# Decode attention over cached keys and values plus a gated MLP: a key load in two transfers, another place for the products with the values, and a finer cut of an output weight

## The chip, the cores and the metric

The kernel runs on one core of a Trainium2 chip. The metric is device time in microseconds (us) of one execution; the kernel before took 668.58, 668.60 and 669.65 us in three timed runs (median 668.6). A separate execution was profiled; its trace is what the views below are taken from.

## The reference

Four decode tokens (batch 4, one position each, width 640) are layer-normalised. Attention with 32 heads of width 128 runs over a cache of 4096 keys and values per head, and a gated MLP over the same normalised input; both results are added to `x`.

```python
def _A_ref(x, k_cache, v_cache, wq, wo):        # x: (4, 1, 640), caches: (4, 32, 4096, 128)
    q = (x @ wq).reshape(B, Sq, Hq, Dh).transpose(0, 2, 1, 3)
    scores = jnp.einsum('bhqd,bhkd->bhqk', q, k) * Dh ** (-0.5)
    p = _softmax(scores, axis=-1)
    o = jnp.einsum('bhqk,bhkd->bhqd', p, v)
    return o.transpose(0, 2, 1, 3).reshape(B, Sq, Hq * Dh) @ wo
...
xn = _layernorm(x, axis=-1)
return x + _A_ref(xn, A_k_cache, A_v_cache, A_wq, A_wo) + _B_ref(xn, B_w_in, B_w_sp, B_b_sp, B_w_out)
```

All tensors are bf16. The two caches are 134 MB each, so almost all of the 282 MB that the kernel reads is keys and values, each read once.

## The kernel before

**Tiles.** The work is cut into `NT` = 16 steps, one for each of four groups of eight heads and each batch. One step's keys are one SBUF tile of 128 partitions x 256 positions x 128 values (`NC` = 256), 8.39 MB, loaded by one transfer (`load_k`, L118); its values are a tile of the same size (`load_v`, L123). Key tiles have two buffers (pool `kp`), value tiles one (pool `vp`). The first key buffer to be used holds `wq` at the start; the value buffer holds the MLP's weights (`w_sb`) at the start and `wo` at the end. The last step's values go to a key buffer as `v_last`, in three transfers.

**One step.** A key tile is worked off in four parts of 64 positions (`NU` = 4). For each part, VectorE multiplies the keys in place by the query (`product`, L402, the line L403), folds the two halves of the 128 products together (`fold`, L410, line L412), TensorE adds up eight slices by eight matmuls against the identity (`sums`, L416, line L421), and VectorE reduces what stands in PSUM to scores (`row_sums`, L429, line L432). The step's softmax is done during the next step: maximum, exponential on ScalarE (`exps`, L488), then on VectorE the spreading of the probabilities into one column block per head (`own_heads`, L497, line L499, tile `pm`), and on TensorE 64 matmuls of `pm` with the value tile (`weighted`, L508, line L514, tile `pv`). `take` (L524) copies the result to SBUF and `diag` (L534) picks each head's rows. After each fourth step a group of heads is divided by its sum and turned (`group_den`, `group_rows`, `group_turn`). At the end `group_proj` multiplies the four groups by the four blocks of `wo` (line L592).

**Order.** The order on TensorE, VectorE, ScalarE and SyncE is the order in which the code calls these functions (`tc.manual_schedule`, L609); nothing is moved by a planner. SyncE issues all large transfers in that order, and a transfer is issued when its buffer is free. In step i, the values of step i are issued after `weighted(i - 1)` has read the one value buffer, and the keys of step i + 2 after the fourth `sums` of step i has read its key buffer. The compiled program counts the landings of its transfers on eight semaphores in turn, so that an issue also waits for the transfer eight issues before it.

**The end.** In the last step the four blocks of `wo` (1280 KB each) are issued in the place of the next values: the first three in one transfer each, the last in four pieces (`WO_CUTS`, L133: 640, 320, 160 and 160 KB). The order on TensorE is then: products with `v_last`, `group_proj(0)`, `diag`, `group_proj(1)`, `group_turn`, `group_proj(2)`, and `group_proj` of the last block in four pieces (L674).

Of the kernel before, what the change touches and what calls it, by code (L numbers as in the profile page):

```python
# [17 lines left out]
def kernel(  # L18
# [14 lines left out]
    nc = tc.nc  # L33
    P = nc.NUM_PARTITIONS
    Bsz, Sq, D = A_x.shape
    _, H, S, Dh = A_k_cache.shape
# [9 lines left out]
    HG = H // HT  # L46
    NT = HG * Bsz
    LN = P // HT
    NC = HT * S // P
# [10 lines left out]
    WJ = HT * Dh // P  # L60
# [19 lines left out]
    def k_slot(name):  # L80
        return kp.tile([P, SLOT], BF16, tag="k", name=name)

    def v_slot(name):
        return vp.tile([P, SLOT], BF16, tag="v", name=name)
# [20 lines left out]
        out=w_out_sb[:, 0:NFF, :], in_=B_w_out[0 : NFF * P].rearrange("(p k) n -> p k n", k=NFF)  # L105
# [3 lines left out]
    def kv_view(cache, i):  # L109
        hg, b = divmod(i, Bsz)  # L110
        return cache[b, HT * hg : HT * (hg + 1)].rearrange("h s d -> (h s) d").rearrange(
            "(p c) d -> p (c d)", c=NC
        )
# [3 lines left out]

    def load_k(i):  # L118
        t = k_slot("k_nat")
        nc.sync.dma_start(out=t[:], in_=kv_view(A_k_cache, i))  # L120
        k_tiles[i] = t[:].rearrange("p (c d) -> p c d", d=Dh)

    def load_v(i, t):  # L123
        cuts = V_CUTS if i == NT - 1 else (0, NC)
        for c0, c1 in zip(cuts, cuts[1:]):
            nc.sync.dma_start(
                out=t[:, c0 * Dh : c1 * Dh], in_=kv_view(A_v_cache, i)[:, c0 * Dh : c1 * Dh]
            )
        v_tiles[i] = t[:].rearrange("p (c d) -> p c d", d=Dh)

    wo_v = A_wo.rearrange("(g p j) n -> g p j n", p=P, j=WJ)
    wo_t = []
    WO_CUTS = (0, 4, 6, 7, WJ)  # L133

    def load_wo():
        t = v_slot("wo")[:, 0 : HG * WJ * D].rearrange("p (g j n) -> p g j n", g=HG, n=D)
        wo_t.append(t)
        for g in range(HG):
            cuts = WO_CUTS if g == HG - 1 else (0, WJ)
            for j0, j1 in zip(cuts, cuts[1:]):  # L140
                nc.sync.dma_start(out=t[:, g, j0:j1, :], in_=wo_v[g][:, j0:j1, :])  # L141

    load_k(0)


# [18 lines left out]
    for i in range(NSTAT):  # L164
# [5 lines left out]
        out=rstd[:], in_=mv[:, 1:2], func=ACT.Sqrt, bias=eps_tile[:Bsz], scale=1.0  # L170
# [3 lines left out]
        out=xn_bf,  # L174
# [9 lines left out]
    for c in range(DC):  # L184
        nc.tensor.transpose(
            out=xnT_ps[:, c, :], in_=xn_v[:, c, :], identity=ident[:Bsz, :Bsz]
# [7 lines left out]
    def out_sum(half):  # L194
        return out_ps[OG * half : OG * half + Bsz, :]

    for half in range(2):
        nc.tensor.matmul(
            out=out_sum(half),
# [9 lines left out]
        out=own[:], in_=ident_f[:].rearrange("p (h l) -> p h l", h=HT), axis=AX.X, op=ALU.add  # L209
# [4 lines left out]
        out=pick[:, :, GW - HT : GW],  # L214
        in_=ident_f[:].rearrange("p (j h c) -> p c h j", c=CB, h=HT),
# [5 lines left out]
        out=row_head_f[:],  # L221
        in_=ident_f[:ROWS, :ROWS].rearrange("p (b h) -> p h b", h=HT),
# [5 lines left out]
        out=row_head[:], in_=row_head_f[:, :, None].to_broadcast([ROWS, HT, LN])  # L228
# [3 lines left out]
        out=row_batch_f[:],  # L232
        in_=ident_f[:ROWS, :ROWS].rearrange("p (b h) -> p b h", h=HT),
# [8 lines left out]
    for h in range(H):  # L242
        for c in range(DC):
            nc.tensor.matmul(  # L244
                out=q_ps[:, h, :],
# [6 lines left out]
    nc.vector.tensor_copy(out=qT[:], in_=q_ps[:])  # L252

    load_k(1)


# [124 lines left out]
    def stage_q(i):  # L381
        hg, b = divmod(i, Bsz)
        q_l = small.tile([P, HT, LN], BF16, name="q_l", bufs=1)
        nc.scalar.copy(  # L384
            out=q_l[:],
            in_=qT[:, HT * hg : HT * (hg + 1), b : b + 1].to_broadcast([P, HT, LN]),
        )
        qb_ps = ps_m.tile([P, Dh], FP32, tag="m", name="qbc_ps")
        nc.tensor.matmul(  # L389
            out=qb_ps[:],  # L390
            lhsT=q_l[:].rearrange("p h l -> p (h l)"),
            rhs=ident[:],
            start=True,
            stop=True,
        )
        qbcs[i] = small.tile([P, Dh], BF16, name="qbc")
        nc.scalar.copy(out=qbcs[i][:], in_=qb_ps[:])

    def part(i, u):
        return k_tiles[i][:, u * UC : (u + 1) * UC, :]  # L400

    def product(i, u):  # L402
        nc.vector.tensor_tensor(  # L403
            out=part(i, u),
            in0=part(i, u),
            in1=qbcs[i][:, None, :].to_broadcast([P, UC, Dh]),
            op=ALU.mult,
        )

    def fold(i, u):  # L410
        t = part(i, u)
        nc.vector.tensor_tensor(  # L412
            out=t[:, :, 0:HD2], in0=t[:, :, 0:HD2], in1=t[:, :, HD2:Dh], op=ALU.add
        )

    def sums(i, u):  # L416
        t = part(i, u)
        s = sums_ps[i, u] = ps_s.tile([P, UC, RW], FP32, name="s_ps")
        n = HD2 // RW
        for g in range(n):  # L420
            nc.tensor.matmul(  # L421
                out=s[:],
                lhsT=ident[:],
                rhs=t[:, :, g * RW : (g + 1) * RW],
                start=(g == 0),
                stop=(g == n - 1),
            )

    def row_sums(i, u):  # L429
        if u == 0:  # L430
            scores[i] = small.tile([P, NC], FP32, name="s_sb", bufs=1)
        nc.vector.tensor_reduce(  # L432
            out=scores[i][:, u * UC : (u + 1) * UC],
            in_=sums_ps.pop((i, u))[:],
            axis=AX.X,
            op=ALU.add,
        )
# [148 lines left out]
        oTs[hg] = const.tile([P, WJ, Bsz], BF16, name=f"oT{hg}")  # L586
        nc.scalar.copy(out=oTs[hg][:], in_=t_ps[:])

    def group_proj(hg, j0=0, j1=WJ):
        for j in range(j0, j1):  # L590
            for half in range(2):
                nc.tensor.matmul(  # L592
                    out=out_sum(half),
                    lhsT=oTs[hg][:, j, :],
                    rhs=wo_t[0][:, hg, j, half * NOH : (half + 1) * NOH],
                    start=False,
                    stop=(hg == HG - 1 and j == WJ - 1),
                )

    def at(i, fn, *args):  # L600
        if 0 <= i < NT:
            fn(i, *args)

    def group(i, fn):
        if 0 <= i < NT and i % Bsz == Bsz - 1:
            fn(i // Bsz)

    E = mybir.EngineType
    with tc.manual_schedule(engines={E.PE, E.DVE, E.Activation, E.SP}):  # L609
        stage_q(0)  # L610
        gmlp()
        load_v(0, v_slot("v_nat"))
        for i in range(NT):
            product(i, 0)
            fold(i, 0)
            at(i - 1, row_sums, NU - 1)
            at(i - 1, lane_max)
            group(i - 2, group_rows)
            sums(i, 0)
            at(i - 1, turn_max)  # L620
            group(i - 2, group_turn)
            product(i, 1)
            at(i - 1, head_max)
            at(i - 1, spread_max)
            fold(i, 1)
            at(i - 1, bias)
            at(i - 1, exps)
            at(i + 1, stage_q)
            sums(i, 1)
            row_sums(i, 0)  # L630
            product(i, 2)
            at(i - 1, own_heads)
            fold(i, 2)
            sums(i, 2)
            row_sums(i, 1)
            at(i - 1, weighted)
            if i == 0:
                pass
            elif i < NT - 1:
                load_v(i, v_slot("v_nat"))  # L640
            else:
                load_wo()
            at(i - 1, take)
            product(i, 3)
            fold(i, 3)
            sums(i, 3)
            row_sums(i, 2)
            if i + 2 < NT:
                load_k(i + 2)
            elif i + 2 == NT:  # L650
                load_v(NT - 1, k_slot("v_last"))
            at(i - 1, diag)
            group(i - 1, group_den)
        L = NT - 1
        row_sums(L, NU - 1)
        lane_max(L)
        group(L - 1, group_rows)
        turn_max(L)
        head_max(L)
        spread_max(L)  # L660
        bias(L)
        exps(L)
        own_heads(L)
        for c0, c1 in zip(V_CUTS, V_CUTS[1:]):
            weighted(L, c0, c1)
        take(L)
        group_den(HG - 1)
        group_proj(0)
        diag(L)
        group_rows(HG - 1)  # L670
        group_proj(1)
        group_turn(HG - 1)
        group_proj(2)
        for j0, j1 in zip(WO_CUTS, WO_CUTS[1:]):  # L674
            group_proj(HG - 1, j0, j1)

        res = small.tile([P, NOH], BF16, tag="two_k", name="res")
        out_v = out.flatten_outer_dims()
        r0, r1 = slice(0, Bsz), slice(OG, OG + Bsz)
        nc.scalar.copy(out=res[r0], in_=out_ps[r0])  # L680
        nc.vector.tensor_copy(out=res[r1], in_=out_ps[r1])
        nc.scalar.dma_start(out=out_v[:, 0:NOH], in_=res[r0])
        nc.sync.dma_start(out=out_v[:, NOH:D], in_=res[r1])
# [30 lines left out]
```

## Time and profile before

| | |
|---|---|
| timed runs | 668.58, 668.60, 669.65 us |
| profiled execution | 669.53 us, of which the span from first to last instruction is 667.8 us |
| VectorE busy | 505.9 us (76%) |
| TensorE matmul busy | 312.8 us (47%) |
| ScalarE busy | 33.6 us (5%) |
| SyncE's DMA queue (q1) | 282.24 MB, busy for 98.2% of the 16 engines' span |
| read from HBM | 282.24 MB, 423 GB/s over the span |
| L403 `product` | 64 of 4417 ns, 282.7 us; idle before them 100.3 us, all of it for key transfers |
| L421 `sums` | 512 matmuls, 201.6 us |
| L412 `fold` | 64 of 2285 ns, 146.2 us |
| L514 `weighted` | 960 matmuls with `v_nat`, 60.8 us |

The busy time of an engine says how much it did, not whether the end waited for it. Which one the end waited for is read from the chain of waits that ended last, and from the share and the rate of the DMA engines in slices of the span. A busy matmul is not TensorE at its peak, since matmuls are pipelined.

### The profile page before, as it was taken

The numbers are of one execution on the slowest core, as the hardware profiler recorded it, in microseconds if no ns is written. First come the engines' busy times: TensorE is split into PE (matmuls) and PEld (weight loads), VectorE is DVE, ScalarE is ACT, GpSimd is POOL, SyncE is SP. The second block draws the span as 40 slices with busy tenths as digits, with TensorE's granted clock in tenths as the row PEclk, the third lists the DMA queues.
The fourth block names the chain that finished last, engine by engine and source line by source line (L and its number), as shares of the span: only waits on it lengthen the run. The fifth ranks groups of instructions, "written<-read, shape, count | busy, mean of one in ns | idle before, by whom it ended". The sixth has DMA issues, their size and how long they took to land.

```text
span 667.8 us, 4772 instructions
## 1 busy us (share of the span) xinstructions
PE 312.8 (47%) x2089; PEld 128.7 (19%) x2089; DVE 505.9 (76%) x328; ACT 33.6 (5%) x93; POOL 1.0 (0%) x8
## 2 busy tenths in 40 slices
PE   0605546524626335462734446272434626444467
PEld 0501112211202112120211212121111212111123
DVE  1239999939689596968969596996949699695971
ACT  0200000000000000000000000000000000000000
POOL 0000000000000000000000000000000000000000
PEclk9999978575766778576665857666576755768688
DMA  9999997999999999999999999999999999999996
GB/s 372 448 437 440 417 412 315 440 437 440 433 436 416 416 441 436 436 433 440 437 432 436 437 420 433 432 424 433 440 437 432 436 440 425 432 436 425 418 417 263
DMA packets 6497, 282.56 MB, mean 423 GB/s; under 512 B 736, under 2 KB 1100, under 8 KB 1484
## 3 DMA queue, kind: packets, MB, share of 16 engines
q1 hardware_dynamic: 6456, 282.24, 98.2%
q8 instruction: 16, 0.26, 0.2%
q14 instruction: 5, 0.04, 0.0%
q10 hardware_dynamic: 20, 0.01, 0.0%
HBM read 282.24 MB, written 0.01 MB: 423 GB/s over the span
## 4 chain that ended last, share of the span: by engine, by line
DMA 54%; DVE 33%; PE 11%; ACT 1%; issue 1%; SPq 1%; DVEq 0%
DMA k_nat<-in_A_k_cache_dram 51%; DVE k_nat L403 19%; DVE k_nat L412 9%; PE s_ps L421 6%; PE pv L514 4%; DMA wo<-in_A_wo_dram 2%; DVE s_sb L432 2%; DVE pm L499 1%; ACT p L488 1%; PE out_ps L592 1%; DVE m L441 1%; DVE wide L565 0%; DVE o_n L559 0%; DVE nm L451 0%; SPq L141 0%
## 5 line engine op out<-in xcount | busy, mean ns | idle before, releaser
L403 DVE TENSOR_TENSOR k_nat<-k_nat,qbc 128x8192 bf16<-128x8192 bf16 x64 | 282.7, 4417 | 100.3 <-DMA k_nat<-in_A_k_cache_dram 100.3
L421 PE MATMUL s_ps<-k_nat,ident 128*128 128x512 bf16 x512 | 201.6, 565 | 257.4 <-DVE k_nat L412 257.4
L412 DVE TENSOR_TENSOR k_nat<-k_nat 128x4096 bf16<-128x4096 bf16 x64 | 146.2, 2285 | 1.2
L421 PEld LDWEIGHTS <-ident 128*128 128x128 bf16 x512 | 65.6, 131 | 371.0 <-issue 285.1
L514 PE MATMUL pv<-v_nat,pm 128*32 128x512 bf16 x960 | 60.8, 410 | 0.0
L432 DVE TENSOR_REDUCE s_sb<-s_ps 128x64 f32<-128x512 f32 x64 | 43.8, 685 | 11.4 <-ACT p L488 10.0
L514 PEld LDWEIGHTS <-pm 128*32 128x32 bf16 x1024 | 26.9, 104 | 45.9 <-issue 22.8
L462 PE MATMUL nb_ps<-nm,ones_row 1*128 1x8 f32 x32 | 7.3, 297 | 32.3 <-DVE nm L451 32.3
L488 ACT ACTIVATE p<-s_sb,nb 128x256 bf16<-128x256 f32 x16 | 8.1, 507 | 279.1 <-DVE nb_h L470 279.1
L389 PE MATMUL qbc_ps<-ident,q_l 128*128 128x128 bf16 x16 | 4.6, 289 | 37.3 <-ACT q_l L384 37.3
L524 ACT COPY e<-pv 128x512 f32<-128x512 f32 x16 | 9.4, 586 | 235.9 <-PE pv L514 229.2
L499 DVE TENSOR_TENSOR pm<-p,own_c 128x2048 bf16<-128x2048 bf16 x16 | 19.5, 1219 | 0.7 <-ACT p L488 0.7
L534 PE MATMUL o_ps<-e,pick 128*32 128x128 f32 x128 | 17.0, 275 | 0.0
L534 PEld LDWEIGHTS o_ps<-e,pick 128*32 128x32 f32 x128 | 12.8, 109 | 6.4 <-issue 6.4
L462 PEld LDWEIGHTS nb_ps<-nm,ones_row 1*128 1x128 f32 x32 | 5.9, 228 | 40.6 <-DVE nm L451 28.6
L252 DVE CAST qT<-q_ps 128x128 bf16<-128x128 f32 x1 | 0.3, 292 | 14.8 <-PE q_ps L244 14.8
L555 DVE RECIPROCAL rden<-den 32x1 f32<-32x1 f32 x4 | 0.6, 156 | 12.5 <-PE den L551 12.5
L244 PE MATMUL q_ps<-xnT,wq 128*128 128x4 bf16 x160 | 4.4, 166 | 11.1 <-DMA wq<-in_A_wq_dram 11.1
L389 PEld LDWEIGHTS <-q_l 128*128 128x128 bf16 x16 | 1.7, 106 | 39.0 <-ACT q_l L384 38.7
L592 PE MATMUL out_ps<-wo,oT 128*4 128x320 bf16 x64 | 6.4, 363 | 1.7 <-DMA wo<-in_A_wo_dram 1.7
L441 DVE TENSOR_REDUCE m<-s_sb 128x1 f32<-128x256 f32 x16 | 6.7, 420 | 0.6
L244 PEld LDWEIGHTS <-wq 128*128 128x128 bf16 x160 | 4.3, 104 | 11.5 <-DMA wq<-in_A_wq_dram 11.5
(85 smaller groups left out, 76.9 us busy)
## 6 DMA issues: line engine op xcount, KB each, us to landing
wq<-in_A_wq_dram SPq DMA_DIRECT2D x1, 5120.0 KB
v_last<-in_A_v_cache_dram SPq DMA_DIRECT2D x1, 4096.0 KB, 34.3
v_last<-in_A_v_cache_dram SPq DMA_DIRECT2D x2, 2048.0 KB, 38.9
wo<-in_A_wo_dram SPq DMA_DIRECT2D x3, 1280.0 KB
w_sb<-in_B_w_in_dram SPq DMA_DIRECT2D x1, 2160.0 KB, 20.1
w_sb<-in_B_w_out_dram SPq DMA_DIRECT2D x1, 960.0 KB, 22.7
wo<-in_A_wo_dram SPq DMA_DIRECT2D x1, 640.0 KB, 16.6
wo<-in_A_wo_dram SPq DMA_DIRECT2D x1, 320.0 KB, 17.0
```

Of the source, the lines that this page charges most:

```text
L403: nc.vector.tensor_tensor(out=part(i, u), in0=part(i, u), in1=qbcs[i][:, None, :].to_broadcast([P, UC, Dh]), op=ALU.mult,)
L412: nc.vector.tensor_tensor(out=t[:, :, 0:HD2], in0=t[:, :, 0:HD2], in1=t[:, :, HD2:Dh], op=ALU.add)
L421: nc.tensor.matmul(out=s[:], lhsT=ident[:], rhs=t[:, :, g * RW : (g + 1) * RW], start=(g == 0), stop=(g == n - 1),)
L432: nc.vector.tensor_reduce(out=scores[i][:, u * UC : (u + 1) * UC], in_=sums_ps.pop((i, u))[:], axis=AX.X, op=ALU.add,)
L441: nc.vector.tensor_reduce(out=m1[:], in_=scores[i][:], axis=AX.X, op=ALU.max)
L462: nc.tensor.matmul(out=nb_ps[:], lhsT=ones_row[:], rhs=maxes[i][:], start=True, stop=True)
L488: nc.scalar.activation(out=probs[i][:], in_=scores.pop(i)[:], func=ACT.Exp, bias=maxes.pop(i)[:], scale=scale_qk, accum_out=accs[hg][:, b ...
L499: nc.vector.tensor_tensor(out=pm[:], in0=probs.pop(i)[:] .rearrange("p (n c) -> p n c", c=CB)[:, :, None, :] .to_broadcast([P, NB, HT, CB] ...
L514: nc.tensor.matmul(out=pvs[i][j * GW : (j + 1) * GW, :], lhsT=pm[:, n, :, :].rearrange("p h c -> p (h c)"), rhs=v_nat[:, n * CB : (n + 1) ...
L524: nc.scalar.copy(out=es[i][:], in_=pvs.pop(i)[:].rearrange("p (c d) -> p c d", d=Dh))
L534: nc.tensor.matmul(out=o_ps[hg][:], lhsT=pick[:, c, GW - HT - HT * b : 2 * GW - HT - HT * b], rhs=e[:, c, :], start=(b == 0 and c == 0), s ...
L592: nc.tensor.matmul(out=out_sum(half), lhsT=oTs[hg][:, j, :], rhs=wo_t[0][:, hg, j, half * NOH : (half + 1) * NOH], start=False, stop=(hg = ...
```

## The change

Three edits, none of which changes what is computed.

1. The keys of step 0 are loaded by two transfers, of the first and of the last 128 positions of each partition, instead of one. Parts 0 and 1 of step 0 need the first transfer only; the compiled program has the product of part 0 wait for the first and that of part 2 for the second.
2. In every step, `weighted(i - 1)` is called right behind `own_heads(i - 1)`, and so stands ahead of `sums(i, 2)` on TensorE. Before it stood behind it. On VectorE nothing changes places.
3. The third block of `wo` is loaded in two transfers of 640 KB. The last block keeps its four pieces; the loop over pieces in the calls of `group_proj` is gone, but its matmuls are issued in the same order.

```diff
     def load_k(i):
         t = k_slot("k_nat")
-        nc.sync.dma_start(out=t[:], in_=kv_view(A_k_cache, i))
+        for c0, c1 in ((0, NC // 2), (NC // 2, NC)) if i == 0 else ((0, NC),):
+            nc.sync.dma_start(
+                out=t[:, c0 * Dh : c1 * Dh], in_=kv_view(A_k_cache, i)[:, c0 * Dh : c1 * Dh]
+            )
...
-    WO_CUTS = (0, 4, 6, 7, WJ)
+    WO_CUTS = ((0, WJ), (0, WJ), (0, 4, WJ), (0, 4, 6, 7, WJ))
...
         for g in range(HG):
-            cuts = WO_CUTS if g == HG - 1 else (0, WJ)
-            for j0, j1 in zip(cuts, cuts[1:]):
+            for j0, j1 in zip(WO_CUTS[g], WO_CUTS[g][1:]):
                 nc.sync.dma_start(out=t[:, g, j0:j1, :], in_=wo_v[g][:, j0:j1, :])
...
             product(i, 2)
             at(i - 1, own_heads)
+            at(i - 1, weighted)
             fold(i, 2)
             sums(i, 2)
             row_sums(i, 1)
-            at(i - 1, weighted)
             if i == 0:
                 pass
             elif i < NT - 1:
...
         group_turn(HG - 1)
         group_proj(2)
-        for j0, j1 in zip(WO_CUTS, WO_CUTS[1:]):
-            group_proj(HG - 1, j0, j1)
+        group_proj(HG - 1)
```

More of the change, by code (lines that the diff above doesn't have):

```diff
@@ L587, in group_turn, with group_proj @@
         nc.scalar.copy(out=oTs[hg][:], in_=t_ps[:])
-    def group_proj(hg, j0=0, j1=WJ):
-        for j in range(j0, j1):
+    def group_proj(hg):
+        for j in range(WJ):
             for half in range(2):
```

## The prediction

> **What bounds the kernel now.** I read the page's slices first (40 of 16.7 us each): the share of time in which the 16 DMA engines were busy, and the rate.
>
> ```profile
> DMA  9999997999999999999999999999999999999996
> GB/s 372 448 437 440 417 412 315 440 437 440 433 436 416 416 441 436 436 433 440 437 432 436 437 420 433 432 424 433 440 437 432 436 440 425 432 436 425 418 417 263
> ```
>
> The engines are at 90% or more everywhere but in slice 7 (100 to 117 us, 315 GB/s) and at the two ends. So the transfers set the pace, and the time is the stream's length plus what it stands idle. VectorE does not set it: of all its waits the largest is for keys,
>
> ```profile
> DVE k_nat L403 <- DMA k_nat<-in_A_k_cache_dram: 100.3, 14, 12.9
> ```
>
> 100.3 us in 14 waits. Second view: busy time by windows, around slice 7 (the last two numbers are DMA share and GB/s).
>
> ```profile
> 80.00:98.00 18.00, 8.49 (x24) 2.97 (x23) 17.33 (x12) 1.05 (x4) 0.00 (x0) 0.80 1.00 433
> 98.00:100.00 2.00, 2.00 (x9) 0.52 (x11) 2.00 (x1) 0.00 (x0) 0.00 (x0) 0.50 0.68 295
> 100.00:102.00 2.00, 2.00 (x32) 0.82 (x28) 1.97 (x2) 0.00 (x0) 0.00 (x0) 0.76 0.03 8
> 102.00:104.00 2.00, 2.00 (x41) 0.81 (x30) 2.00 (x3) 0.00 (x0) 0.00 (x0) 1.00 0.00 0
> 104.00:106.00 2.00, 2.00 (x11) 0.87 (x11) 2.00 (x2) 0.59 (x1) 0.00 (x0) 1.00 1.48 524
> ...
> 180.00:600.00 420.00, 193.69 (x1147) 76.33 (x1145) 337.18 (x197) 18.00 (x57) 0.00 (x0) 0.67 1.00 434
> ```
>
> From 100 to 104 us nothing is moved; from 180 to 600 us the stream holds 434 GB/s with a share of 1.00. There is one hole, of some 5 us. Why it is there is in the DMA queue's issues in order of time and in the chain of waits, at the same place:
>
> ```profile
> 75.73 0.33 SPq L120 DMA_DIRECT2D k_nat<-in_A_k_cache_dram  x1
> 104.02 0.33 SPq L126 DMA_DIRECT2D v_nat<-in_A_v_cache_dram  x1
> 105.83 0.33 SPq L120 DMA_DIRECT2D k_nat<-in_A_k_cache_dram  x1
> ```
> ```profile
> 3.23 40.89 DMA k_nat<-in_A_k_cache_dram
> 44.14 4.44 DVE k_nat L403
> ...
> 92.89 1.13 DVE pm L499
> 94.02 2.21 DVE k_nat L412
> 96.23 0.04 issue
> 96.28 3.57 PE s_ps L421 x8
> 99.85 4.12 PE pv L514 x45
> 103.97 1.85 PE s_ps L421 x8
> 105.82 0.02 issue
> 105.83 40.92 DMA k_nat<-in_A_k_cache_dram
> ```
>
> After the keys of step 2 (issued at 75.73) the queue holds nothing until the values of step 1 are issued at 104.02. They wait for the one value buffer, read to its end by `weighted(0)` at 104.0, which stood behind `sums(1, 2)` (3.57 us from 96.28), though its operand `pm` was ready at 94.02. And all of this hangs on step 0, which began at 44.14, when the whole 8.39 MB of its keys had landed. In later steps the values come in time: step 4's are issued at 216.83, and the keys ahead of them land at 180.50 + 43.65 = 224.15 (chain), 7.3 us later.
>
> **Size of the hole.** By the windows 60 to 100, 100 to 105 and 105 to 140 us (425, 43 and 439 GB/s): 40 x 425 + 5 x 43 + 35 x 439 = 32,580 kB against 80 x 434 = 34,720; the difference is 4.9 us. By slice 7: (437 - 315) / 437 x 16.7 = 4.7 us. By the trace's landing records, one for each engine: the keys of step 2 landed from 100.55 to 102.17, the values of step 1 from 125.24 to 125.98, and a tile of 8.39 MB takes 19.35 us (the last landings of two neighbours, 166.12 and 185.46, for instance); the earliest engine lost 125.24 - 100.55 - 19.35 = 5.3 us, the latest 4.5. Bounds 4.5 to 5.3; I take 5.2, nearer the upper end, because the engines that are late in the end (last landing of `wo` 664.08, first 660.59) were late after the hole, not before it.
>
> **Edit 1, keys of step 0 in two.** The first half lands half a tile earlier, 44.12 - 9.7 = 34.4 us. VectorE is free (its last MLP instruction ends at 31.2) and so is TensorE (33.3). Step 0's parts 0 and 1 take 58.16 - 44.14 = 14.0 us, to 48.4, when the second half has been there since 44.1. Step 0 then ends at 34.4 + (72.68 - 44.14) = 63.0; the keys of step 1 land at 44.12 + 19.35 = 63.5, so step 1 begins 72.68 - 63.5 = 9.2 us earlier. Costs: one more issue on SyncE (0.33 us) ahead of step 1's keys, which wait until 20.7 for the query matmuls, so nothing; packets of 32 KB instead of 64 KB, 2 x 1.213 against 2.418 us in the packet records, eight per engine: 0.06 us on the stream.
>
> **Edit 2, `weighted` ahead of `sums(i, 2)`.** TensorE's in-order queue now has `weighted(i - 1)` wait for `pm`, with `sums(i, 2)`, `sums(i, 3)` and `diag` behind it. It starts at 94.02 - 9.2 = 84.8 in step 1. Values of step 0 landed at 63.5 + 19.35 = 82.8, two us before. Its duration: 3.73 us where it followed 3.57 us of matmuls (640.02), 5.32 us where TensorE had idled 2.2 us before (650.24); the new place has an idle time of 94.0 - 91.3 = 2.7 us ahead, so 5.3. Step 1's values are issued at 90.1 instead of 104.02, when the stream still has some 10 us of step 2's keys. The hole closes. From the new position alone (without edit 1) the issue would be at 99.4, just where the stream dries up; from edit 1 alone at 94.8, early enough. The two overlap: the hole is paid back once, and either edit gets most of it. `sums(i, 2)` ends at 94.0 + 5.3 + 1.9 to 3.6 (clock full, as in 103.97, or half, as in 96.28) = 101.2 to 102.9 on the old scale, and `row_sums(i, 2)`, which needs it, comes at 103.4: no wait on VectorE. `sums(i, 3)` follows `fold(i, 3)` at 103.4 instead of `weighted` at 103.97; after 0.5 to 2.2 us of idleness it may fall from 1.9 to 3.6 us, so the next keys are issued 0.5 us earlier to 1.2 later. They stand behind 19 us of values; nothing comes of it. In steady steps the transfers are issued 12 instead of 7 us ahead of need, worth nothing.
>
> **Edit 3, third `wo` block in two.** The end before:
>
> ```profile
> 645.33 15.57 DMA wo<-in_A_wo_dram
> 660.90 0.04 issue
> 660.95 3.94 PE out_ps L592 x32
> ```
>
> 32 matmuls follow the landing of the third block at 660.90, while the last piece landed at 664.08 (landing records) and the last matmul began at 664.54. TensorE is 0.4 us behind the stream. With the first half landing 1.5 us sooner, eight matmuls go ahead of 660.9 and the rest catches up: gain 0 to 0.4 us. Against it: if the last `sums` takes 3.6 us, the closing chain (maximum, exponentials, `pm`, products, `diag`, `group_rows`, `group_turn`, ready at 659.7 now) is 1.7 us later, 661.4, and with 32 matmuls at 0.133 us (their spacing after 660.95) ends 1.1 us later than now; at 0.078 us (their spacing at 657.83) it still ends with the stream. Bounds -0.4 to +1.1; I take -0.2, since TensorE would come to them out of 10 us of work. Eight packets more per engine cost 0.07 us; the eighth piece waits for the third transfer of `v_last` (some 650), 10 us before the stream ends.
>
> **Sum.** -5.2 + 0.06 + 0.07 - 0.2 = -5.3 us: span 667.8 to 662.5, the profiled execution 669.53 to 664.2. That execution was 0.9 above the median of the timed runs (668.6), so the median should be 663.3.
>
> **A rule that speaks against it.** The trace prices a further transfer at nearly nothing: the first piece of `v_last` (4096 KB) lands 34.3 us after issue, the next (2048 KB, issued 0.4 us later) 38.9, so 4.9 us for what 434 GB/s moves in 4.8. The Trainium skill, "DMA: Bandwidth & Descriptors", section "Anatomy of one DMA", puts about 2 us fixed on each transfer beside its bytes (fitted on another issuing path); if that held the queue, the two added transfers would give back 4 us and the time would be 667.3.
>
> **Rivals.**
> - *The hole closes but engines stay uneven* (0.10). The hole let the early engines wait for the late ones: spread 1.6 us before it, 0.7 after. Without it lateness adds up; 16 single packets of instructions (queue q8 on the page) hit engines singly, each about 1.5 us (landings of step 3's keys spread 2.2 us after one at 137.6). If the last engine is hit once more: gain 5.3 - 1.5 = 3.8, 664.8; twice: 666.3. For it: the spread did grow to 3.5 by the end. Against: before had the same packets on the same engines after the hole.
> - *Each added transfer holds the queue for its round trip* (0.02). The lone 5 KB load of `x`, issued at 0.74, let VectorE go at 2.27 (timeline): 1.5 us. Two of that give back 3.0: 666.3. The `v_last` rows speak against it.
> - *Nothing comes of it* (0.05): the closing chain, not the stream, sets the end. Before, that chain was ready 1.2 us ahead of the third block; it would have to be 5 us later relative to the stream: 668 or so.
> - *Slower* (0.04): `weighted` at its new place waits for values and holds `sums(i, 2)` back. Values of step 2 landed at 135.09 + 31.0 = 166.1, `pm` is ready at 168.3: 2.2 us in hand. VectorE feels it once values are 2 to 4 us late, and a step (33.2 us of work in 38.7) outlasts the transfers only from some 7 us late. At 8 us late in 14 steps: about 14 x 0.9 - 5.3, 675 to 676. For it: the wait is now ahead of two `sums`. Against: keys and values land 19.35 us apart whatever is edited, since the stream is one queue.
>
> **Chances and range.** Forecast 0.79 (662.3 to 664.6 for it alone); the rivals as given. Less than 0.2% (1.3 us) cannot be told from no change here, the three timed runs spreading by 1.1. Faster 0.91, same 0.05, slower 0.04. The range 662.2 to 665.4 takes in the hole's bounds, the closing chain's +1.1, half of the first rival and part of the runs' spread.
>
> **What would show it.** Product of part 0 begins near 34.4; no window at 0 GB/s between 60 and 140 us, and slice 7 at 430 or more; step 1's values issued near 90; every `wo` landing 5 us earlier; first products with values some 2 us behind their landing. Wrong: a hole at another place, VectorE's waits for keys falling away (it would be the bound), or `weighted` waiting for value transfers.

## The result and the profile after

The changed kernel took 663.81 us (median of 6 runs, 663.66 to 664.02), the kernel before, run beside it, 669.06 (6 runs, 668.34 to 669.66): ratio 0.9922, 95% interval 0.9909 to 0.9935. The forecast was 663.3. The profiled execution took 663.72 us with a span of 661.9, against 669.53 and 667.8; in the trace's own figures the spans are 661.95 and 667.75, 5.8 us less.

The slices of the changed kernel's page, 16.5 us each:

```profile
DMA  8999999999999999999999999999999999999996
GB/s 370 427 447 416 440 437 436 441 432 416 445 432 436 433 440 424 437 428 432 433 436 433 436 432 425 440 433 428 436 437 432 440 424 433 432 433 440 416 414 282
```

The slice that had 315 GB/s is gone (436 now); what stays below 410 is the first and the last. The same windows as before, with DMA share and GB/s at the end of each row:

```profile
core 0: us, PE busy (x) PEld busy (x) DVE busy (x) ACT busy (x) POOL busy (x), PEclk, DMA share, GB/s
80.00:98.00 18.00, 11.71 (x89) 4.24 (x88) 15.38 (x7) 0.58 (x1) 0.00 (x0) 0.80 1.00 431
98.00:100.00 2.00, 1.03 (x9) 0.76 (x8) 0.00 (x0) 0.00 (x0) 0.00 (x0) 1.00 0.83 360
100.00:102.00 2.00, 0.00 (x0) 0.00 (x0) 0.00 (x0) 0.00 (x0) 0.00 (x0) 0.73 1.06 459
102.00:104.00 2.00, 0.00 (x0) 0.10 (x1) 1.36 (x1) 0.00 (x0) 0.00 (x0) 0.50 1.14 492
104.00:106.00 2.00, 0.00 (x0) 0.00 (x0) 2.00 (x1) 0.00 (x0) 0.00 (x0) 0.50 1.06 459
```

Where the DMA engines moved 8 and 0 GB/s (100 to 104 us) they now move 459 and 492 (a packet counts where it starts, so short windows swing about 434). The idle time has moved to the compute engines: from 100 to 102 us none of them has work (0.00 each), since step 1 is done and the keys of step 2 have not landed. The issues of SyncE and the chain, at the same place:

```profile
66.03 0.33 SPq L121 DMA_DIRECT2D k_nat<-in_A_k_cache_dram  x1
89.10 0.33 SPq L129 DMA_DIRECT2D v_nat<-in_A_v_cache_dram  x1
98.07 0.33 SPq L121 DMA_DIRECT2D k_nat<-in_A_k_cache_dram  x1
```
```profile
3.02 31.40 DMA k_nat<-in_A_k_cache_dram
34.42 0.02 issue
34.44 4.44 DVE k_nat L405
...
66.03 36.52 DMA k_nat<-in_A_k_cache_dram
```

Step 0 begins at 34.44 instead of 44.14, and step 1's values are issued at 89.10 instead of 104.02, while the keys of step 2 land only at 66.03 + 36.52 = 102.55. The chain now runs through this stage by way of a transfer that was queued long before. In the trace's landing records the values of step 1 land from 120.01 to 121.90 (125.24 to 125.98 before), and the last piece of `wo` at 658.62 (664.08): the stream ends 5.46 us sooner. From that landing to the end of the span it takes 3.33 us instead of 3.68; the two gains, 5.46 and 0.35, are the 5.8 us.

Two waits of the changed kernel (engine, line, what it waited for; total, times, longest):

```profile
DVE k_nat L405 <- DMA k_nat<-in_A_k_cache_dram: 92.4, 16, 7.2
PE pv L516 <- DVE pm L501: 38.9, 16, 3.3
```

VectorE still waits for keys, so it has not become the bound. The moved products wait for their own operand `pm` and in no step for the values.

### The profile page after: what moved, and what is told of

It reads as the page before. It is cut to its first block, busy times and chain, and to the rows that moved or that the text cites. A ratio compares the mean times of both kernels' runs of the same rounds, so it can differ in the third digit from the quotient of the medians.

```text
span 661.9 us, 4774 instructions
## 1 busy us (share of the span) xinstructions
PE 319.8 (48%) x2089; PEld 132.8 (20%) x2089; DVE 506.1 (76%) x328; ACT 33.6 (5%) x93; POOL 1.0 (0%) x8
## 4 chain that ended last, share of the span: by engine, by line
DMA 59%; DVE 36%; PE 3%; ACT 1%; SPq 0%; issue 0%; DVEq 0%
DMA k_nat<-in_A_k_cache_dram 50%; DVE k_nat L405 21%; DVE k_nat L414 11%; DMA v_last<-in_A_v_cache_dram 7%; PE s_ps L423 3%; DVE s_sb L434 2%; DMA wo<-in_A_wo_dram 2%; DVE pm L501 1%; ACT p L490 1%; DVE m L443 0%; DVE nm L453 0%; SPq L107 0%; SPq L129 0%; DVE nb_h L472 0%; DVE res L682 0%
## 5 line engine op out<-in xcount | busy, mean ns | idle before, releaser
L423 PE MATMUL s_ps<-k_nat,ident 128*128 128x512 bf16 x512 | 187.2, 532 | 207.8 <-DVE k_nat L414 207.8
L423 PEld LDWEIGHTS <-ident 128*128 128x128 bf16 x512 | 62.2, 125 | 309.3 <-issue 234.5
L516 PE MATMUL pv<-v_nat,pm 128*32 128x512 bf16 x960 | 77.7, 495 | 36.7 <-DVE pm L501 36.7
L516 PEld LDWEIGHTS <-pm 128*32 128x32 bf16 x1024 | 32.5, 122 | 95.2 <-DVE pm L501 51.5
L536 PE MATMUL o_ps<-e,pick 128*32 128x128 f32 x128 | 20.7, 315 | 0.0
L536 PEld LDWEIGHTS o_ps<-e,pick 128*32 128x32 f32 x128 | 14.8, 126 | 10.3 <-issue 9.3
L516 PE MATMUL pv<-v_last,pm 128*32 128x512 bf16 x64 | 6.4, 591 | 2.2 <-DVE pm L501 2.2
```

Source lines behind the costliest of these rows:

```text
L423: nc.tensor.matmul(out=s[:], lhsT=ident[:], rhs=t[:, :, g * RW : (g + 1) * RW], start=(g == 0), stop=(g == n - 1),)
L516: nc.tensor.matmul(out=pvs[i][j * GW : (j + 1) * GW, :], lhsT=pm[:, n, :, :].rearrange("p h c -> p (h c)"), rhs=v_nat[:, n * CB : (n + 1) ...
L536: nc.tensor.matmul(out=o_ps[hg][:], lhsT=pick[:, c, GW - HT - HT * b : 2 * GW - HT - HT * b], rhs=e[:, c, :], start=(b == 0 and c == 0), s ...
```

## The experiments

The first four ran side by side with 15 runs of the kernel before (median 669.34, 668.27 to 670.47), the last three with 7 (669.35, 668.18 to 670.05).

**Edit 1 alone.** Only `load_k` is changed, as in the diff above.

> Edit 1 alone (keys of step 0 in two transfers). Theory (one hole, paid back once): step 0 begins near 34.4 us, step 1's values are issued near 95, some 5 us before the stream would dry up near 100; no hole between 95 and 107 us, so nearly the whole gain: 4.9 to 5.5 us under the kernel before. Rival (the edits add up, each in proportion to how much earlier it brings the issue, 9.2 and 4 to 6 us): 3.2 us under it, with a hole of some 2 us left.

Measured: 663.57 us (4 runs, 663.50 to 663.73), ratio 0.9912 (0.9897 to 0.9927): 5.8 us under the kernel before.

```profile
95.42 0.33 SPq L129 DMA_DIRECT2D v_nat<-in_A_v_cache_dram  x1
```

Step 1's values are issued at 95.42 and land from 119.85 to 121.76, 19.36 us behind the keys ahead of them (100.49 to 102.40). No hole is left, and the whole gain is there, a little over what was expected. The rival's 3.2 us is ruled out.

**Edit 2 alone.** Only the call of `weighted` is moved.

> Edit 2 alone (products with the values ahead of the third part's sums). Theory: the products begin at 94.0 and take 3.6 to 6.5 us, step 1's values are issued at 97.7 to 100.5; the stream's keys end near 100 and a transfer needs some 0.9 us from issue to its first packet, so what is left is a hole of 0 to 2 us: 3.1 to 5.3 us under the kernel before. Rival (the edits add up): 1.9 us under it.

Measured: 664.70 us (5 runs, 664.45 to 665.67), ratio 0.9932 (0.9919 to 0.9944): 4.6 us under. The products took 4.92 us (on TensorE from 94.12), and the issue came at

```profile
99.09 0.33 SPq L126 DMA_DIRECT2D v_nat<-in_A_v_cache_dram  x1
```

with landings from 120.59 to 123.06, so a hole of 0.7 us is left for the earliest engine and of 1.4 for the last (less the 19.35 us of a tile and the keys' landings, 100.58 to 102.33). 5.8 and 4.6 make 10.4, while both edits together make 5.3 to 5.6: the hole is paid back once.

**Edit 3 alone.** Only `WO_CUTS` and `load_wo` are changed.

> Edit 3 alone (third wo block in two transfers). Theory: the hole stays, TensorE starts on the third block 1.5 us sooner and ends with the stream: 0 to 0.4 us under the kernel before. Rival (each added transfer holds the queue for its round trip of 1.5 us): 1 us over it.

Measured: 669.49 us (11 runs, 668.80 to 670.05), ratio 1.0002 (0.9994 to 1.0011). Nothing comes of it, and it costs nothing. TensorE did start on the third block sooner, at 659.97, and in its profile the time from the last `wo` landing (664.66) to the end was 3.30 us, against 3.68 in the profile of before. The next run shows that this is not the edit's doing.

**Edits 1 and 2, without edit 3.**

```diff
-    WO_CUTS = ((0, WJ), (0, WJ), (0, 4, WJ), (0, 4, 6, 7, WJ))
+    WO_CUTS = ((0, WJ), (0, WJ), (0, WJ), (0, 4, 6, 7, WJ))
```

> Edits 1 and 2 without edit 3. Theory: no hole, 4.9 to 5.4 us under the kernel before; the changed kernel's edge over it is edit 3's 0 to 0.4 us, seen in the time from the last landing of wo to the end (3.7 us here, 3.3 in the changed kernel). Rival (edit 3's transfer costs the queue 1.5 us): 6.5 us under the kernel before.

Measured: 663.77 us (4 runs, 663.43 to 664.00), ratio 0.9914 (0.9901 to 0.9928), the same as the changed kernel. Its time from last landing (658.83) to the end is 3.30 us, with the third block in one transfer. TensorE's matmuls with `wo` in this run, in order of time:

```profile
655.68 1.25 PE L594 MATMUL out_ps<-wo,oT 128*4 128x320 bf16 x16 [1.57 <-DMA wo<-in_A_wo_dram]
657.22 1.95 PE L594 MATMUL out_ps<-wo,oT 128*4 128x320 bf16 x16 [0.29 <-DMA wo<-in_A_wo_dram]
```

The third block's 16 matmuls take 1.25 us after an idle time of 1.57, where before they took 2.1 (0.133 us each) after 1.47. The granted clock was 1.00 here from 656 to 658 us, and 0.50 before from 661 to 664 us. So the 0.35 us at the end were a matter of the clock that TensorE was granted in the one profiled execution of before, and not of the second transfer.

**A longer hole: the first products later.** In the kernel before, for step 1 alone:

```diff
-            at(i - 1, weighted)
+            if i != 1:
+                at(i - 1, weighted)
-            if i == 0:
+            if i < 2:
                 pass
...
-            at(i - 1, take)
+            if i != 1:
+                at(i - 1, take)
...
             sums(i, 3)
             row_sums(i, 2)
+            if i == 1:
+                at(0, weighted)
+                load_v(1, v_slot("v_nat"))
+                at(0, take)
```

> The kernel before, with the products with the first values put later, behind the fourth part's sums, in step 1 alone. Theory (every us of hole goes to the end): the products begin at 105.4 to 107.1 us and take 3.6 to 6.5, so step 1's values are issued at 109.0 to 113.6 instead of 104.0, the hole is 5 to 9.6 us longer and the kernel as much slower, us for us. Rival (later steps have room that takes it up): less than half of the added hole is found in the time.

Measured: 675.97 us (4 runs, 675.31 to 676.99), ratio 1.0103 (1.0086 to 1.0120), 6.6 us over the kernel before.

```profile
110.36 0.33 SPq L126 DMA_DIRECT2D v_nat<-in_A_v_cache_dram  x1
```
```profile
100.00:105.00 5.00, 1.47 (x4) 0.55 (x4) 4.97 (x4) 0.00 (x0) 0.00 (x0) 0.78 0.00 0
105.00:110.00 5.00, 5.00 (x69) 2.07 (x67) 4.97 (x2) 0.00 (x0) 0.00 (x0) 0.87 0.01 3
```

In the profiles the issue comes 6.34 us later than before (110.36 against 104.02), the last `wo` landing 6.33 us later (670.41 against 664.08). Nothing after it takes any of the hole up.

**The new order in step 1 alone.** In the kernel before, `weighted` stands ahead of `fold(i, 2)` for i = 1 and behind `sums(i, 2)` else.

> The kernel before with the products ahead of the third part's sums in step 1 alone. Theory (only the hole counts): as with the new order in all steps, values of step 1 issued at 97.7 to 100.5, 3.5 to 5.3 us under the kernel before, and within 0.5 us of the run with the order changed in all steps. Rival (the new order gives something in every step): 1 us or more over that run.

Measured: 664.41 us (4 runs, 664.22 to 664.80), ratio 0.9929 (0.9915 to 0.9944), 0.3 us from edit 2 in all steps. Only the place in step 1 counts; in the other steps the transfers are queued in time with either order.

**All key and value tiles in two transfers.** The changed kernel with

```diff
-        for c0, c1 in ((0, NC // 2), (NC // 2, NC)) if i == 0 else ((0, NC),):
+        for c0, c1 in ((0, NC // 2), (NC // 2, NC)):
...
-        cuts = V_CUTS if i == NT - 1 else (0, NC)
+        cuts = V_CUTS if i == NT - 1 else (0, NC // 2, NC)
```

> The changed kernel with every key and value tile in two transfers, 30 more. Theory (a further transfer costs eight packets of 0.008 us on each DMA engine): 30 x 0.06 = 1.9 us over the changed kernel, some 3.4 us under the kernel before. Rival (each transfer holds the queue for 1.5 us or more): 45 us or more over the changed kernel. It could also be faster, if earlier starts of the steps were worth anything; by theory they are not.

Measured: 666.02 us (4 runs, 665.81 to 666.35), ratio to the kernel before 0.9952 (0.9935 to 0.9968), 2.2 us over the changed kernel. The packets of the queue took 658.20 us on each engine (their sum divided by 16) against 655.10: 0.10 us for each of the 30 further transfers. This kernel also shows the mechanism of the slower rival, since its steps begin with half a key tile and so reach their products before the values are there:

```profile
PE pv L516 <- DMA v_nat<-in_A_v_cache_dram: 57.9, 14, 5.7
...
DVE s_sb L434 <- PE s_ps L423: 49.5, 15, 4.7
```

TensorE waits 57.9 us for values, VectorE 49.5 us for the sums behind them, and yet the time grew by no more than the packets did. The stream was full all the while (431 GB/s from 180 to 600 us).

## Why the prediction was right

- **The bound and the hole.** That the stream of transfers sets the time, us for us, is shown by four kernels with one end and different holes. Issue of step 1's values and last landing of `wo`: 95.42 and 658.41 (edit 1), 99.09 and 659.59 (edit 2), 104.02 and 664.08 (before), 110.36 and 670.41 (products late). Past 99 us, 11.27 us of later issue cost 10.82 us of later landing.
- **Size of the hole.** Taken as 5.2 (bounds 4.5 to 5.3). The first engine's last landing moved from 660.59 to 655.31, 5.28 us, the last engine's by 5.46, a little over the upper bound. The excess comes from the engines' lag. The spread of the landings grew from 0.7 us behind the hole to 3.5 at the end before, and from 1.9 to 3.3 in the changed kernel, so the last landing came 4.1 us sooner at the hole's place and a further 1.4 by the end. The spread at the end is 3.3 to 4.4 us in the profiles without a hole, so a part of the gain hangs on chance. A hole also costs more than its idle time: the first packet of each engine behind it took 2.59 to 3.44 us (mean 2.96), where a packet of 64 KB in the full stream takes 2.42.
- **Edit 1.** First half at 34.4, measured 34.42. What its packets cost does not show: the packets of the queue took 654.89 us on each engine with this edit alone, and 655.49 before, slow first packets behind the hole included.
- **Edit 2.** Products in step 1 at 84.8, measured 85.41. They took 3.64 us where 5.3 was taken, and between 3.64 and 6.47 over the 16 steps; so the issue came at 89.1 instead of 90.1. Neither matters, with more than 10 us in hand. "Either edit gets most of it" held: 5.8 and 4.6 us alone, 5.3 to 5.6 together. In the changed kernel edit 2 does nothing that edit 1 had not done.
- **Edit 3.** The step that failed in its reason: "gain 0 to 0.4 us", of which 0.2 was taken, by TensorE catching up. A gain of 0.35 us appeared at that place, but runs without the edit have it too, and the edit alone measured 1.0002. No run shows this term as an effect of the edit.
- **Sum.** 5.3 us was forecast for the profiled executions, 5.8 measured: the stream ended 5.46 us sooner where 5.2 - 0.13 = 5.07 was put, the end took 0.35 less where 0.2 was put. Against the first three runs (668.6) the change is 4.8, against the six beside it 5.25, against the 15 later ones 5.5. The median of three had been low, which is why the forecast time of 663.3 lies half a us under the measured one. That 5.3 comes so near to 5.25 is in part luck: it holds 0.2 us of edit 3 that are not there, and a hole that was taken too small.
- **Rivals.** *Uneven engines:* the spread of the last piece's landings is 3.3 us, against 3.5 before, so lateness was not added. It can be: the run with the new order in step 1 alone has 4.4 us there, and ended 1.1 us behind the changed kernel in its profile (last landing 659.77), though its values landed as early as with edit 1 (120.05 to 121.69). *A price on each transfer:* 0.10 us for one more in a full queue, not 1.5. The Trainium skill, "DMA: Bandwidth & Descriptors", section "Anatomy of one DMA", gives about 2 us for the fixed part of a transfer, fitted on another issuing path; no such price shows in these runs. *The closing chain* did not move the end: 3.24 to 3.33 us from the last landing to the end in the changed kernel and all seven variants. *Slower by waiting for values:* the moved products had their values in every step; where they were made to wait, it stayed within the room of a step.

No version beat the changed kernel clearly. Edit 1 alone (663.57) does the same with one loop.

## What to carry to other kernels

In a kernel that is bound by transfers, look for the slices in which the DMA engines have nothing queued, and follow the one late issue back to what holds its buffer: 5 us in one place decided here, and the 15 other steps did not matter. Two edits that close the same hole do not add up, so price them against what is left. Splitting one transfer so that work starts on its first half is cheap (0.1 us for one more in a full queue) and brings forward everything behind it, but it pays only where the queue would otherwise run dry.

## What was not expected

The kernels with the hole vary more from run to run: 668.27 to 670.47 us before (15 runs), 668.80 to 670.05 with edit 3 alone, 675.31 to 676.99 with the longer hole, against 663.50 to 663.73 with edit 1 alone and 663.66 to 664.02 with the change. A likely reason, argued and not shown: with the hole, the end hangs on the duration of one burst of 64 matmuls in step 1; without it, on nothing but the stream. That the burst varies is shown: it took 3.64 us in the changed kernel at a granted clock of 1.00, 4.19 before at 0.86, 4.92 with edit 2 alone at 0.73, and 5.32 with all tiles in two transfers at 0.68.

The 16 DMA engines do not end together. In the changed kernel the last piece of `wo` landed between 655.31 and 658.62; in every profile 16 single packets of 16 KB of instructions run on another queue and take about 1 us each, and the spread of a tile's landings grows at some of them (before, from 2.1 to 3.65 us with the packet at 492.2 us). That is 3.3 us at the end in which part of the engines are idle, and it was left as it is.
